# One core: q and k of eight early attention tiles come two tiles to a transfer and are turned by unit products

## The chip, the cores and the metric

The kernel runs on one core of a Trainium2 chip. The metric is the device time of one execution in microseconds (us), as a median of several runs. The engines are named as in the profile: PE (matrix products), DVE, ACT and POOL (elementwise work), SP (issues the transfers). "Granted clock" is the share of full speed that PE was given.

## The reference, cut to what matters

```python
# q, k, v: (8 batches, 8 heads, 576 tokens, 64)
scores = scale * q @ k.T                       # scale = 1/8
scores = where(0 <= row - col < 64, scores, -1e9)   # a token sees itself and 63 before it
attn = exp(scores - max); attn = attn / (sum + 1e-9)
x = (attn @ v) as (8, 576, 512)                # heads side by side
mixed = real(fft(fft(x, axis=1), axis=2))
u = x + mixed
un = (u - mean) / sqrt(var + 1e-6)             # per token
out = u + maximum(un @ w_ch1, 0) @ w_ch2       # 512 -> 2048 -> 512
```

## The kernel before

**Tiles.** The 8 x 576 tokens are cut into 36 tiles of 128 tokens, nine to a pair of batches. Tile 4 of a pair holds the last 64 tokens of one batch and the first 64 of the next. A tile goes through attention (`attn_tile`), its output is combined into four parts (`y`), turned, and folded into two transform stages for each batch (`fft`: tiles `pg`, `pz`), then normalized (`norm_tile`) and put through the two layers in chunks of two tiles (`ffn`, later `ffn7`: tiles `ph` and `po`, by far most of PE's work).

**Plain tiles.** Tiles 0 to 10 (`T < PRO`) are computed in whole 32-bit numbers, the others in pairs of 16-bit parts. For a plain tile `attn_tile` does this:

- `load` (line 538) brings k, q and v, each 128 tokens on 128 partitions, 8 heads of 64 numbers. In the source one token of one head is 256 contiguous bytes. The tiles `kn`, `qn` come from a ring of two; for odd tiles the second halves of `qbd` (`qbuf`) are used.
- `flip` (line 574) turns k and then q with four 128-column PE transposes each, into the PSUM tiles `pk` and `pq`; a copy (line 506 on ACT, line 510 on DVE) brings them into `kst` (three slots of one tile each) and `qbd` (two slots).
- `score` (line 662, tile `psc`) needs this tile's q, its k, and the k of the tile before it. Then masking on DVE (677), exponent on ACT (685), the turn of the result (696, `pp`, copied to `pt`), the product with v (739, `pa`, v in `va` and `ve`), and the division (747 to 758, into `xu`).

**Weights.** Both weight matrices come as 32 transfers of 512 KB (line 1277), each partition's piece being 4 KB contiguous, into `room` or `flex`, and DVE turns each two of them into `ws` by three instructions (1289, 1294, 1301). The slots of `ws` are free until then.

**Order.** Every step is recorded by `op` with the buffers that it reads and writes (`Buf`), which gives its dependences in the order of recording. The order of execution is then a table written into the source, `ORDER`; `SECOND` names the steps that run on their second engine. Each engine goes through its list strictly in order. All these loads are issued by SP. Where the planner's arithmetic sees PE idle for over 0.8 us before the first layer work, `WARM` has it fill the gap with products that nothing reads (line 1759, tile `warm`).

Of the kernel before, what the change touches and what calls it, by code (L numbers as in the profile page):

```python
# [27 lines left out]
P = 128  # L28
# [370 lines left out]
def attn_fft_ffn_kernel(ctx: ExitStack, tc: tile.TileContext, q, k, v, w1, w2, gidx, dft_d, dft_s, mask, out):  # L399
# [120 lines left out]
    def attn_tile(T, base):  # L520
# [36 lines left out]
        def keys(h, jj, rows):  # L557
# [6 lines left out]
            step = old - own  # L564
            return halves[rows, own : old + (1 if step > 0 else -1) : step]

        if whole:
            bpk, bpq = Buf("ps"), Buf("ps")

            def flip(dst, src):  # L570
# [1137 lines left out]
    for nth, (x, j) in enumerate(W_ORDER):  # L1708
        weight_pair(x, j, nth)
# [81 lines left out]
```

## Time and profile before

| what | value |
|---|---|
| median of 3 runs | 942.68 us (942.63 to 948.22) |
| the profiled execution, its own time | 945.16 us |
| its span, first to last instruction | 943.4 us |
| PE busy | 924.2 us (98%) |
| DVE, ACT, POOL busy | 705.3, 435.1, 441.5 us |
| warm products among PE's instructions | 45, the last at 40.9 us |

The span is what the rows divide up; 1.8 us of the execution's own time lie outside it, and this execution is 2.5 us above the median of the runs. The share of busy time is an average over stages: at the start, in the tail and in the middle PE waits for different things.

### The profile page before, as it was taken

The numbers are of one execution on the slowest core, as the hardware profiler recorded it, in microseconds if no ns is written. First come the engines' busy times: TensorE is split into PE (matmuls) and PEld (weight loads), VectorE is DVE, ScalarE is ACT, GpSimd is POOL, SyncE is SP. The second block draws the span as 40 slices with busy tenths as digits, with TensorE's granted clock in tenths as the row PEclk, the third lists the DMA queues.
The fourth block names the chain that finished last, engine by engine and source line by source line (L and its number), as shares of the span: only waits on it lengthen the run. The fifth ranks groups of instructions, "written<-read, shape, count | busy, mean of one in ns | idle before, by whom it ended". The sixth has DMA issues, their size and how long they took to land.

```text
span 943.4 us, 24809 instructions
## 1 busy us (share of the span) xinstructions
PE 924.2 (98%) x9717; PEld 703.2 (75%) x9717; DVE 705.3 (75%) x1982; ACT 435.1 (46%) x979; POOL 441.5 (47%) x823
## 2 busy tenths in 40 slices
PE   7799999999999999999999999999999999999998
PEld 6677777666766676666766676667779998888887
DVE  5898998887767866677658757888898965675664
ACT  6875777834555424445443543444334442422111
POOL 2653464744744555465746544655601454124012
PEclk9999999999999999999999999999999999999999
DMA  9997447999689969879979788785402032210100
GB/s 231 239 263 202 133 144 147 167 173 169 136 193 163 198 122 167 185 152 207 197 168 190 150 162 169 163 147 108 137 12 57 24 96 65 68 35 13 57 24 23
DMA packets 300230, 128.69 MB, mean 136 GB/s; under 512 B 277768, under 2 KB 278152, under 8 KB 300112
## 3 DMA queue, kind: packets, MB, share of 16 engines
q1 hardware_dynamic: 297248, 118.06, 59.6%
q0 software_dynamic: 2720, 8.92, 3.3%
q8 instruction: 76, 1.25, 0.6%
q14 instruction: 42, 0.34, 0.1%
q10 hardware_dynamic: 144, 0.13, 0.0%
HBM read 60.76 MB, written 19.94 MB: 86 GB/s over the span
## 4 chain that ended last, share of the span: by engine, by line
PE 83%; DMA 5%; DVE 4%; POOL 3%; SPq 2%; issue 2%; ACT 1%; POOLq 0%; DVEq 0%; ACTq 0%
PE ph L1419 22%; PE po L1400 22%; PE ph L1573 13%; PE po L1548 11%; PE pz L1061 3%; PE pg L1023 3%; PE pa L739 3%; PE psc L662 2%; DMA kn<-in_k 1%; POOL flex L516 1%; DMA ve<-va 1%; DMA qn<-in_q 1%; DMA pt<-flex 1%; SPq L1277 1%; PE py L850 1%
## 5 line engine op out<-in xcount | busy, mean ns | idle before, releaser
L1400 PE MATMUL po<-ws,hh 128*128 128x512 f16 (+1 forms) x1116 | 284.5, 391 | 0.5 <-issue 0.2
L1419 PE MATMUL ph<-room,ws 128*128 128x256 f16 x2112 | 256.1, 273 | 1.8 <-DVE hh L1431 1.8
L1419 PEld LDWEIGHTS <-ws 128*128 128x128 f16 x2112 | 205.3, 98 | 54.1 <-issue 2.8
L1400 PEld LDWEIGHTS <-hh 128*128 128x128 f16 x1056 | 101.1, 98 | 90.0 <-DVE hh L1431 0.7
L1573 PE MATMUL ph<-room,ws 128*128 128x256 f16 x1152 | 136.2, 273 | 0.0
L1573 PEld LDWEIGHTS <-ws 128*128 128x128 f16 x1152 | 112.6, 98 | 13.6
L1428 ACT ACTIVATE hh<-ph 128x512 f16<-128x512 f32 x88 | 52.3, 594 | 120.8 <-PE ph L1419 99.8
L685 ACT ACTIVATE pr<-pr,nm 128x128 f32<-128x128 f32 x288 | 91.2, 393 | 31.5 <-DVE nm L677 31.4
L1431 DVE SCALAR_TENSOR_TENSOR hh<-ph,hh 128x512 f16<-128x512 f32 x88 | 60.4, 686 | 36.6 <-ACT hh L1428 36.5
L1135 POOL DMA_INDIRECT mt<-md,gix x34 | 42.0, 1235 | 96.7 <-DVE mv L1163 81.5
L677 DVE CUSTOM_DVE_ANT_0 pr<-psc,mskb 128x128 f32<-128x128 f32 x288 | 65.0, 287 | 25.9 <-PE psc L662 19.7
L1584 ACT ACTIVATE hx<-ph 128x512 f32<-128x512 f32 x47 | 27.8, 595 | 113.3 <-PE ph L1573 103.7
L1589 DVE TENSOR_TENSOR hx<-hx 128x128 f32<-128x128 f32 x164 | 45.1, 318 | 37.8 <-ACT hx L1584 36.2
L1548 PEld LDWEIGHTS <-hh 128*128 128x128 f16 x658 | 64.4, 98 | 7.6
L1597 POOL TENSOR_TENSOR hl<-hx,hh 128x256 f16<-128x256 f32 (+1 forms) x40 | 28.0, 730 | 77.3 <-DVE hh L510 53.7
L516 POOL TENSOR_TENSOR up<-un,up 128x128 f16<-128x128 f32 x84 | 40.9, 516 | 46.3 <-ACT up L506 38.8
L516 POOL TENSOR_TENSOR flex<-pr,flex 128x128 f16<-128x128 f32 x92 | 42.5, 494 | 36.2 <-ACT flex L506 18.2
L1548 PE MATMUL po<-ws,hh 128*128 128x256 f16 x282 | 51.2, 273 | 0.0
L1597 DVE TENSOR_TENSOR hl<-hx,hh 128x896 f16<-128x896 f32 x37 | 40.4, 1097 | 7.8 <-ACT hh L506 6.5
L752 POOL TENSOR_TENSOR rc<-rc,mone 128x4 f32<-128x4 f32 x29 | 32.5, 1129 | 26.6 <-DVE rc L747 16.8
L739 PE MATMUL pa<-ve,pt 128*64 128x65 f16 (+1 forms) x776 | 37.0, 203 | 2.5 <-ACT ve L506 1.8
L1548 PE MATMUL po<-ws,hl 128*128 128x256 f16 x141 | 38.4, 273 | 0.0
(244 smaller groups left out, 1718.6 us busy)
## 6 DMA issues: line engine op xcount, KB each, us to landing
room<-in_moe_w_ch SPq DMA_DIRECT2D x20, 512.0 KB
flex<-in_moe_w_ch SPq DMA_DIRECT2D x12, 512.0 KB
ve<-va SPq DMA_DIRECT2D x47, 130.0 KB
flex<-in_v SPq DMA_DIRECT2D x22, 256.0 KB
xs<-xu SPq DMA_DIRECT2D x22, 256.0 KB
xv<-xs SPq DMA_DIRECT2D x22, 256.0 KB
out<-xv SPq DMA_DIRECT2D x21, 256.0 KB
md<-mp SPq DMA_DIRECT2D x24, 192.0 KB
```

Of the source, the lines that this page charges most:

```text
L516: eng.tensor_tensor(out=out[:, k : k + w], in0=in0[:, k : k + w], in1=in1[:, k : k + w], op=al)
L677: nc.vector.tensor_tensor_reduce(out=t["pr", g][:, hp], in0=t["ps", g][:, hp], in1=mskb[:, m : m + P], scale=-0.125, scalar=3.0e38, op0=AL ...
L685: nc.scalar.activation(pr, pr, AF.Exp, bias=t["nm", g][:, hp : hp + 1], scale=-1.0)
L739: nc.tensor.matmul(pa[sl, hp], pt[:, sl], v_, start=(x == 0), stop=(x == len(mm) - 1))
L1400: nc.tensor.matmul(t["po"][i], l_, r_, start=(f == 0 and x == 0), stop=(f == NKF - 1 and x == len(mm) - 1))
L1419: nc.tensor.matmul(ph, l_, r_, start=(x == 0), stop=(x == len(mm) - 1))
L1428: nc.scalar.activation(t["hh", j][:, 0], ph, AF.Relu)
L1431: nc.vector.scalar_tensor_tensor(out=hh[:, 1], in0=ph, scalar=0.0, in1=hh[:, 0], op0=ALU.max, op1=ALU.subtract)
L1548: nc.tensor.matmul(t["po", bk][:, x], t["h", j][a][:, slot], right(n, j, b_), start=(j == 0 and k == 0 and n in opens), stop=(j == seven - ...
L1573: nc.tensor.matmul(ph, l_, r_, start=(x == 0), stop=(x == len(mm) - 1))
L1589: eng.tensor_tensor(out=x[:, o], in0=x[:, p0], in1=x[:, p1], op=al)
L1597: eng.tensor_tensor(out=lo[:, a:b_], in0=x[:, a + 1 : b_ + 1], in1=hi[:, a:b_], op=ALU.subtract)
```

## The change

For tiles 0 to 3 and 5 to 8 (`twin`), two neighbouring tiles of one batch (0 and 1, 2 and 3, 5 and 6, 7 and 8) share one transfer of k and one of q (`two_tiles`). A partition receives two neighbouring tokens of each head, 512 contiguous bytes in the source, in 1024-number pieces of two `ws` slots (14 to 17 or 28 to 31, tile name `ws`). Since tokens 2p and 2p+1 then lie on one partition, the turn is done for even and for odd tokens apart (`turn_two`): per head one product with 64 stationary columns of data and the 128 x 128 unit matrix as moving operand, 8 products for one call, head by head into the lower and the upper 64 rows of the PSUM tile (`pt0...`, printed as `pt`). `spread_two` copies the result with a step of two columns into `kst` (both tiles' slots) or into both q slots. Each pair of tiles thus has 2 transfers in place of 4, 4 calls of `turn_two` in place of 4 of `flip`, and 4 copies as before. A pair's q needs both q slots free and a pair's k two of the three k slots.

The recording of weights, of the first layer chunk and of the normalization of tiles 0 to 8 moves behind tile 8, so that the weights' use of `ws` is ordered after the new use. `ORDER` and `SECOND` are new. Everything from about PE's row 2,470 of 17,388 on stands as before but for a few swaps.

```diff
-    qbuf = [cp.tile([P, 1024], F32, name=f"qbd{i}") for i in range(2)]
+    qboth = cp.tile([P, 2, 1024], F32, name="qbd")
+    qbuf = [qboth[:, i] for i in range(2)]
...
+        twin = T < NT and n != 4
+        if not twin:
+            bk, bq = Bkq if i else (Buf("kq"), Buf("kq"))
+            op("DMA", 1.45, base - 8, lambda: load("kn", "kq", k), writes=[bk], lat=2.0)
+            op("DMA", 1.45, base - 8, lambda: load("qn", "kq", q), writes=[bq], lat=2.0)
...
-        if whole:
+        if twin and n in (0, 2, 5, 7):
+            slot = (14, 30)[n in (2, 7)]
+            def two_tiles(x, src):
+                b_, s0 = b0 + P * n // S, P * n % S
+                rows = src[b_, :, s0 : s0 + 2 * P, :].rearrange("h (p i) d -> p h (i d)", i=2)
+                at = slot + (2 if slot == 14 else -2) * x
+                t["two", x] = ws[:, at : at + 2].rearrange("p i c -> p (i c)").rearrange("p (h i d) -> p h i d", h=H, i=2)
+                nc.sync.dma_start(t["two", x].rearrange("p h i d -> p h (i d)"), rows)
+            def turn_two(x, odd):
+                t["pt2", x, odd] = bank("ps", f"pt{x}{odd}_{T}")
+                for h in range(H):
+                    rows = slice(64 * (h % 2), 64 * (h % 2) + 64)
+                    nc.tensor.matmul(
+                        t["pt2", x, odd][rows, h // 2], t["two", x][:, h, odd], ident, start=True, stop=True
+                    )
+            def spread_two(eng, x, odd):
+                if x == 0:
+                    a, b_ = T % 3, (T + 1) % 3
+                    dst = kst.rearrange("p x (a s) -> p x a s", a=4)[:, a : b_ + 1 if b_ > a else None : b_ - a]
+                else:
+                    dst = qboth[:, :, 0:512].rearrange("p x (a s) -> p x a s", a=4)[:, :: 1 if i == 0 else -1]
+                copy(eng, dst[..., odd::2], t["pt2", x, odd].rearrange("p a (x s) -> p x a s", x=2))
+            for x, src in enumerate((k, q)):
+                bw = Bws[slot + (2 if slot == 14 else -2) * x :][0:2]
+                to = [BkT[T % 3], BkT[(T + 1) % 3]] if x == 0 else [Bq[0], Bq[1]]
+                op("DMA", 2.2, base - 8, lambda x=x, src=src: two_tiles(x, src), writes=bw, lat=2.0)
+                for odd in range(2):
+                    bpt2 = Buf("ps")
+                    op("PE", 1.0, base + 0.5 * x, lambda x=x, odd=odd: turn_two(x, odd), [*bw, Bid], [bpt2])
+                    op("ACT", 0.48, base + 0.1 + 0.5 * x, lambda e, x=x, odd=odd: spread_two(e, x, odd), [bpt2], to,
+                       alt=("DVE", 0.6), port=False)
+        elif twin:
+            pass
+        elif whole:
...
-        if T == 4:
+        if T == 8:
+            for nth, (x, j) in enumerate(W_ORDER):
+                weight_pair(x, j, nth)
+            for args in norms[:4]:
+                norm_tile(*args)
...
-1 115 0 9 7 116 3 15 118 119 120 145 121 124 144 129 16 149 125 130 173 126 131 147 150 117 127 148 17 132 21 18 176 153
...
```

Of the instructions, 64 one-record transposes (`pk`, `pq`; 16 calls of `flip`) become 128 unit products (16 calls of `turn_two`), and the 45 warm products become 28. In the changed file the lines are 538 and 578 (loads one by one, and by two), 584 (`turn_two`), 614 (`flip`), 702, 736, 779, 890 (scores, `pp`, `pa`, `py`), 1317 (weights) and 1806 (warm).

First SP, from its first transfer, before (`kn`, `qn` and `qbd` are the loads of k and q of tiles 0, 1 and 2; `room` is a weight transfer):

```order
L538 DMA kn_102<-in_k 128x8x64
L538 DMA qn_110<-in_q 128x8x64
L470 DMA mskb<-in_mask 128x384
L1277 DMA room<-in_moe_w_ch 128x1024
L538 DMA qbd_79<-in_q 128x8x64
L538 DMA qbd_78<-in_k 128x8x64
L1277 DMA room<-in_moe_w_ch 128x1024
L538 DMA kn_189<-in_k 128x8x64
L538 DMA va_82<-in_v 128x8x64
L1277 DMA room<-in_moe_w_ch 128x1024
L538 DMA qn_253<-in_q 128x8x64
```

The same stretch of SP now (the `ws` loads are of tiles 0 and 1, then of 2 and 3):

```order
L578 DMA ws<-in_k 128x8x128
L578 DMA ws<-in_q 128x8x128
L1317 DMA room<-in_moe_w_ch 128x1024
L470 DMA mskb<-in_mask 128x384
L578 DMA ws<-in_k 128x8x128
L1317 DMA room<-in_moe_w_ch 128x1024
L538 DMA va_81<-in_v 128x8x64
L538 DMA va_82<-in_v 128x8x64
L1317 DMA room<-in_moe_w_ch 128x1024
L578 DMA ws<-in_q 128x8x128
```

The q of tiles 2 and 3 stands behind both v loads and the third weight transfer, where the q of tile 2 alone stood behind one v load and the third weight transfer.

Then PE between the scores of tile 0 and those of tile 1, before:

```order
L574 MATMUL pq_175<-ident,qbd_79 128x128 x4
...
L696 MATMUL pp_1_197<-ident,pr_1_147 128x128 x4
L574 MATMUL pk_203<-ident,qbd_78 128x128 x4
L696 MATMUL pp_0_210<-ident,pr_0_145 128x128 x4
...
L574 MATMUL pk_226<-ident,kn_189 128x128 x4
L662 MATMUL psc_0_232<-kst,qbd_79 64x128 x2
```

The same stretch of PE now, up to the first product with v and the turns behind it (tile 1 needs no load and no turn of its own any more):

```order
L584 MATMUL pt_2_197<-ident,ws 64x128 x8
...
L736 MATMUL pp_1_225<-ident,pr_1_173 128x128 x4
...
L736 MATMUL pp_0_236<-ident,pr_0_171 128x128 x4
L702 MATMUL psc_0_245<-kst,qbd 64x128 x2
...
L779 MATMUL pa_0_271<-ve_83,pt_0_237 64x65
...
L584 MATMUL pt_2_302<-ident,ws 64x128 x8
L584 MATMUL pt_2_322<-ident,ws 64x128 x8
L584 MATMUL pt_2_340<-ident,ws 64x128 x8
```

The three flips between the two scores have gone; one turn of the next pair's k stands there, and its other three stand behind tile 0's product with v.

## Rows read from the trace of the kernel before

**Rows 1.** The page: span, PE's busy time, granted clock in 40 slices.

```profile
span 943.4 us, 24809 instructions
...
PE 924.2 (98%) x9717; PEld 703.2 (75%) x9717; DVE 705.3 (75%) x1982; ACT 435.1 (46%) x979; POOL 441.5 (47%) x823
...
PEclk9999999999999999999999999999999999999999
```

**Rows 2.** Stretches: each engine's busy us (instructions), granted clock, DMA share, GB/s.

```profile
core 0: us, PE busy (x) PEld busy (x) DVE busy (x) ACT busy (x) POOL busy (x), PEclk, DMA share, GB/s
0.00:8.20 8.20, 6.25 (x58) 4.83 (x58) 0.00 (x0) 2.46 (x3) 1.50 (x13) 1.00 0.80 184
8.20:50.00 41.80, 33.05 (x501) 25.40 (x498) 35.46 (x150) 34.21 (x87) 21.63 (x37) 1.00 1.05 254
50.00:200.00 150.00, 148.56 (x1302) 107.05 (x1302) 133.23 (x348) 106.81 (x230) 81.89 (x126) 1.00 0.71 170
90.00:110.00 20.00, 20.00 (x88) 14.44 (x86) 19.55 (x35) 12.95 (x26) 4.67 (x8) 1.00 0.39 132
```

**Rows 3.** The same stretches, the warm products of line 1759 alone.

```profile
0.00:8.20 8.20, 4.18 (x18) 2.39 (x18) 1.00 0.80 184
8.20:50.00 41.80, 4.63 (x27) 2.23 (x27) 1.00 1.05 254
```

**Rows 4.** PE's waits, 0 to 50 us: us in total, times, longest.

```profile
PE pa L739 <- ACT ve L506: 1.8, 3, 1.1
PE py L850 <- DVE y L516: 1.7, 2, 1.4
PE pk L574 <- DMA kn<-in_k: 1.5, 2, 1.3
PE psc L662 <- ACT qbd L506: 1.2, 2, 0.7
```

**Rows 5.** Timeline of PE: start us, us, instructions, [idle before, releaser].

```profile
4.45 1.06 PE L574 MATMUL pk<-ident,kn 128*128 128x128 f32 x4
...
7.19 1.10 PE L662 MATMUL psc<-kst,qbd 64*64 64x128 f32 x32 [0.46 <-ACT qbd L506]
...
9.49 0.63 PE L574 MATMUL pq<-ident,qbd 128*128 128x128 f32 x4 [0.77 <-DMA qbd<-in_q]
...
10.18 0.60 PE L696 MATMUL pp<-ident,pr 128*128 128x128 f32 x4
...
13.48 0.63 PE L574 MATMUL pk<-ident,kn 128*128 128x128 f32 x4 [1.28 <-DMA kn<-in_k]
...
17.72 0.63 PE L574 MATMUL pq<-ident,qn 128*128 128x128 f32 x4 [0.41 <-DMA qn<-in_q]
...
31.89 0.63 PE L574 MATMUL pk<-ident,kn 128*128 128x128 f32 x4 [0.18 <-DMA kn<-in_k]
```

**Rows 6.** Timeline of SP from 90 to 110 us: transfers issued.

```profile
91.23 0.80 SPq L1277 DMA_DIRECT2D room<-in_moe_w_ch  x2
96.26 0.81 SPq L1277 DMA_DIRECT2D flex<-in_moe_w_ch  x2
99.48 0.33 SPq L1277 DMA_DIRECT2D room<-in_moe_w_ch  x1
```

**Rows 7.** Chain that ended last, 46 to 92 us: start us, us, instructions.

```profile
48.81 1.03 PE psc L662 x32
...
51.82 1.08 PE pa L739 x32
...
59.73 0.44 PE pq L574 x4
...
88.93 1.73 PE ph L1419 x8
```

**Rows 8.** Groups by line and shape, 0 to 100 us: busy us, mean ns, idle.

```profile
L506 ACT COPY kst<-pk 128x512 f32<-128x512 f32 x11 | 6.4, 585 | 6.3 <-PE pk L574 6.2
...
L510 DVE COPY qbd<-pq 128x512 f32<-128x512 f32 x1 | 0.7, 692 | 0.1
```

More of the change, by code (lines that the diff above doesn't have):

```diff
@@ L538, in load @@
                 nc.sync.dma_start(t[nm][o : o + m], ap)
-        (bk, bq), bv = Bkq if i else (Buf("kq"), Buf("kq")), Bfl[3]
-        op("DMA", 1.45, base - 8, lambda: load("kn", "kq", k), writes=[bk], lat=2.0)
-        op("DMA", 1.45, base - 8, lambda: load("qn", "kq", q), writes=[bq], lat=2.0)
+        twin = T < NT and n != 4
+        bv = Bfl[3]
+        if not twin:
+            bk, bq = Bkq if i else (Buf("kq"), Buf("kq"))
+            op("DMA", 1.45, base - 8, lambda: load("kn", "kq", k), writes=[bk], lat=2.0)
+            op("DMA", 1.45, base - 8, lambda: load("qn", "kq", q), writes=[bq], lat=2.0)
         if whole:
@@ L1464, in attn_fft_ffn_kernel @@
         half[:, 4:6].rearrange("p i c -> p (i c)"),
-        *(b_[:].bitcast(F16) for b_ in qbuf),
+        *(b_.bitcast(F16) for b_ in qbuf),
         kst16[:, 0 : 2 * 1024],
@@ L1705, in ffn7 @@
             op("DMA", 0.75, -11, lambda g=g: nc.sync.dma_start(of[P * g : P * g + P], xts[g]), [b_], lat=2.0)
-    for nth, (x, j) in enumerate(W_ORDER):
-        weight_pair(x, j, nth)
-    made, behind = 0, {}
+    made, behind, norms = 0, {}, []
     for T in range(NTT):
@@ L1725, in attn_fft_ffn_kernel @@
                 else:
-                    norm_tile(*args)
-        if T == 4:
+                    norms.append(args)
+        if T == 8:
[3 more added lines that the diff above has]
+                norm_tile(*args)
+            del norms[:4]
             for c in range(PLAIN):
@@ L1734, in attn_fft_ffn_kernel @@
                     weight_split(x, j, W_SPLIT + W_STEP * 2 * (8 * x + j))
-        if n in (4, 8):
+        if n in (4, 8) and T > 4:
+            plan.slack = SLACK if T >= NT else 0.0
+            for args in norms:
+                norm_tile(*args)
+            norms.clear()
             plan.slack = FSLACK
```

276 rows, old and new, of tables (ORDER, SECOND) are left out of this document.

## The prediction

> **What bounds the kernel now.** I read the page first [rows 1]: a span of 943.4 us, 924.2 us of PE work, and the granted clock at full speed in every slice. Then the stretches [rows 2] say where PE is not the bound. In its first 50 us PE is idle for (8.20 - 6.25) + (41.80 - 33.05) = 10.7 us; from 50 to 200 us for 1.4 us. Against the span PE is idle for 943.4 - 924.2 = 19.2 us in all, so 8.5 us lie behind 50 us. In the first 50 us PE is also busy with warm products for 4.2 + 4.6 = 8.8 us [rows 3]. Empty time of the start, idle and warm together, is thus 6.1 us up to 8.2 us and 13.4 us from there to 50 us: 19.5 us. That is all that an earlier arrival of q and k can give back; behind 50 us PE has work queued whatever arrives.
>
> What PE waits for there is mixed [rows 4]: loads (k 1.5 us; one of q, 0.8 us, stands in [rows 5]), the copies of turned q on ACT (1.2 us), copies of v (1.8 us), and `y` on DVE (1.7 us). The transfer engines are full from 8 to 50 us (share 1.05), but DVE and ACT are busy for 35.5 and 34.2 of those 41.8 us as well [rows 2].
>
> **The queue.** From 90 to 110 us SP issues only five weight transfers [rows 6], and the engines' share is 0.39 [rows 2]: 0.39 x 20 / 5 = 1.56 us of all 16 engines for 512 KB in 4 KB pieces. Between the products that waited for tile 1's q, tile 2's k and tile 2's q, 4.0 and 4.2 us pass [rows 5], and each time, by SP's order shown with the change, the queue holds two loads of 256 KB and one weight transfer. One load of 1,024 pieces of 256 bytes so takes (4.1 - 1.56) / 2 = 1.27 us: 20 ns for a piece on one engine, against 195 ns for a piece of 4 KB. No row shows 512 bytes. On the straight line between the two prices a piece of 512 bytes takes 31.5 ns and a pair's transfer 2.02 us; at the 4 KB rate it would be 24.4 ns and 1.56 us. It replaces two loads, 2.54 us, so one of the eight new transfers frees 0.5 to 1.0 us of the queue, 4 to 8 us together. I take the straight line, since both ends of it are rows. The Trainium skill (DMA: Bandwidth & Descriptors, Specifications) says that pieces below 512 bytes miss the line rate because each is read and written back; by it the new transfers would cost the lower price and the queue would gain the 8 us. No run here shows it, and by the sum below the whole difference of 4 us in the queue is worth at most as much on PE.
>
> **Part 1, turns: PE work added.** A flip takes 0.44 us [rows 7]; 16 of them go: -7.0 us. A unit product is a plain 32-bit product, which the trace shows as two records: in the first layer 4 products of 256 columns are 8 records in 1.73 us [rows 7], 0.216 us for a record, 0.108 us for one of 128 columns. Alone, a call of 8 products would take 16 x 0.108 = 1.73 us. But the heads alternate between the two column halves, as the products with v do: those, with 64 stationary columns and 65 moving ones, take 1.08 us for 16 products in 32 records, 0.034 us a record where one alone would be 0.055. Perfect halves give 0.86 us for a call; scaling the product with v by columns (0.54 x 128 / 65) gives 1.06 us. The scores, with four places side by side, also need 1.03 / 32 = 0.032 us a record, so 0.033 us looks like a floor for small products, above which 0.054 us lies. I take 0.90 us. Added: 16 x 0.90 = 14.4 us. Together **+7.4 us** (16 x 0.42 = 6.7 to 16 x 0.62 = 9.9); without any overlap it would be +20.6 us. All of it lies on PE's own path; it is free only where it fills empty time.
>
> **Part 2, the first pair.** The first flip before stands at 4.45 us [rows 5], behind warm products. With 2.02 in place of 1.27 us, tiles 0 and 1's k is there at about 5.2 us and their q at 7.2 us. Two turns end at 9.0 us, the copy of q (0.69 us on DVE [rows 8]) at 9.7 us, and the scores run to about 10.8 us, where they ended at 8.2 us [rows 5]. Of these 10.8 us PE works 4 x 0.90 + 1.03 = 4.6 us, so 6.2 us stay empty against 6.1 us before. From scores to the first turned result 2.0 us pass (8.2 to 10.18 [rows 5]), of which one turn of the next k now fills 0.9 us. Tile 1 then needs neither load nor turn; its scores start after the two `pp` (0.9 and 0.4 us) at about 10.8 + 2.0 + 1.3 = 14.1 us, where the 13.48 us load let them start at 14.0 us [rows 5]. So the late start costs nothing from tile 1 on.
>
> **Part 3, the rest of the start.** Up to tile 2's q, which landed at 17.7 us [rows 5], SP's order before has 7 loads and 3 weight transfers, 7 x 1.27 + 3 x 1.56 = 13.6 us of queue; now it has 4 pair transfers, 2 loads and 3 weight transfers up to the q of tiles 2 and 3, 13.5 to 15.3 us: it lands at 17.6 to 19.4 us. Behind it come two weight transfers, tile 4's q, 0.5 MB of constants and tile 4's k, 2 x 1.56 + 2 x 1.27 + 1.5 = 7.2 us: 24.8 to 26.6 us against 31.9 us [rows 5]. Tiles 5 and 6, behind two v loads and two weight transfers, are there at 33.6 to 36.3 us. From tile 4 on the data is 5 us and more ahead, and PE meets its queued work from about 37 us instead of 50. What stays: a wait of up to 2 us for tiles 2 and 3, about 1 us in each of tiles 0, 2 and 3 between scores and turned results, where there is nothing else to do, and some of the waits for v and `y`, which the change doesn't touch. I put the empty time between 10.8 and 50 us at 5 us (2 to 9) in place of 13.4: **-8.4 us** (-11.4 to -4.4).
>
> **What costs nothing.** The copies stay 16; a stepped destination has no row, but ACT takes 585 ns for a contiguous one [rows 8] and 16 x 0.1 us would be spread over engines that do not end the stretch alone. The wait for both q slots holds back only the copies, with ACT and DVE's next steps behind them: the odd tile's scores are by then issued. The weights' move in the recording frees nothing and binds only four late transfers to the turns.
>
> **Sum.** +7.4 - 8.4 = -1.0 us on the span of 943.4: 942.4 us, and 944.2 us for that execution's own time, which lay 2.5 us above the median. On the median: 942.68 - 1.0 = **941.7 us**. The ends of the terms give 943.4 - 4.7 to 943.4 + 5.5, on the median 938.0 to 948.2.
>
> **Rivals.**
> 1. *The queue decides all of the start* (faster). If 512 bytes go at the 4 KB rate and the waits for v and `y` shrink with it, the 13.4 us fall to 1 us and a turn to 0.86 us: -12.4 + 6.7 = -5.7, and with another 1.5 us from the waits behind 50 us 935.5 us. For it: the share of 1.05 to 50 us. Against it: DVE and ACT are over 80% busy there, and DVE for 133 of the next 150 us [rows 2], so that work that arrives sooner finds them taken.
> 2. *The two column halves don't overlap* (slower). At `turn_two` PE then needs 1.73 us a call: +20.6 - 8.4 = +12.2, 954.9 us. It decides from a call of 0.44 + 8.4 / 16 = 0.97 us on; above that the change loses whatever the queue gains. Against it: the product with v has the same stationary shape and alternates in the same way, and overlaps.
> 3. *No relief.* The transfer is still cut into 256-byte pieces, or 512 bytes cost the double: the change then doesn't do what it says, the empty time stays at 19.5 us, and the turns are paid in full: 950.1 us. For it: nothing shows such a piece here. Against it: both sides of the transfer have 512 contiguous bytes.
> 4. *PE's strict order.* A turn stands ahead of tile 0's `pp`, three ahead of tile 1's; when a pair's load is late, everything behind waits though it could go. A queue that falls 2 us further behind costs up to 2 us at each of the two places: 945.7 us, inside the forecast's range.
>
> **How the numbers follow.** The forecast, with rival 4, has 0.69; rival 1 0.12; rival 3 0.10; rival 2 0.06; something else 0.03. Forecast and rival 1 hold 0.81 from 935.5 to 948.2 us; the bounds of the terms take in part of rival 3, so the range is 935 to 949 us. A measurement of this kernel can tell about 1%, 9.4 us, from no change. Even an empty time of zero behind the first 6 us would give -13.4 + 6.7 - 1.5 = -8.2 us, so faster by over 1% has 0.04; slower by over 1% is rival 2, the upper part of rival 3 and some of the rest, 0.10; within 1% 0.86.
>
> **What would show it.** In the changed profile: 8 transfers of 512 KB, DMA's packets below 512 bytes fewer by 16,384 and 8,192 of 512; records of the unit products starting about 0.055 us apart, a call 0.9 us; first scores ending near 11 us, tile 1's starting near 14 us; tile 4's k turned before 28 us; idle and warm together near 11 us in the first 50; and PE idle for less than 3 us from 50 to 200 us. I am wrong if a call takes over 1 us, if the pair's q of tiles 2 and 3 lands past 20 us, or if PE idles for more than 1 us at a time behind 50 us, for then DVE, not PE, sets that stretch.

## The result and the profile after

The changed kernel takes **948.12 us** (median of 20 runs, 944.74 to 953.76) where the kernel before takes 942.65 (20 runs): the ratio is 1.0053, 95% interval 1.0035 to 1.0071, some 5 us slower. I had forecast 941.7, 1 us faster. The size lies inside my range and inside the 1% that I gave 0.86; the sign is wrong.

The page of the changed kernel, span, engines and granted clock as in [rows 1]:

```profile
span 946.9 us, 25106 instructions
...
PE 931.3 (98%) x9892; PEld 709.1 (75%) x9892; DVE 710.2 (75%) x1984; ACT 432.6 (46%) x974; POOL 440.2 (46%) x814
...
PEclk9999999999999999999999999999999999999999
```

Its stretches, columns as in [rows 2], with 50 to 90 us apart (that row of the kernel before stands below them):

```profile
0.00:8.20 8.20, 6.78 (x64) 5.37 (x66) 0.00 (x0) 2.41 (x3) 1.64 (x14) 1.00 0.80 226
8.20:50.00 41.80, 35.76 (x609) 28.63 (x608) 34.55 (x147) 31.04 (x80) 22.58 (x36) 1.00 1.11 280
50.00:90.00 40.00, 38.00 (x398) 30.34 (x391) 33.41 (x97) 27.37 (x72) 29.57 (x45) 0.96 0.58 163
50.00:200.00 150.00, 147.48 (x1332) 106.55 (x1325) 131.70 (x327) 104.72 (x229) 88.33 (x133) 0.99 0.64 155
```

```profile
50.00:90.00 40.00, 39.64 (x406) 31.02 (x406) 36.11 (x125) 27.69 (x73) 22.06 (x34) 1.00 0.86 233
```

The warm products alone, now line 1806, split at the end of the first scores (compare [rows 3]):

```profile
0.00:10.80 10.80, 4.42 (x20) 1.00 0.87 255
10.80:50.00 39.20, 1.38 (x8) 1.00 1.11 275
```

The start did what it was to do. In the first 50 us PE is idle for 7.5 us and warm for 5.8 us, 13.3 us empty where it was 19.5 before; the transfer engines move 280 GB/s from 8 to 50 us where they moved 254. The new loss stands in the third row: from 50 to 90 us, where PE was idle for 0.4 us before, it is idle for 2.0 us, and the granted clock is 0.96 on average. PE's timeline has the two places where it waits longest, and the turns (compare [rows 5]):

```profile
5.38 4.03 PE L584 MATMUL pt<-ident,ws 128*64 128x128 f32 x64
10.29 1.10 PE L702 MATMUL psc<-kst,qbd 64*64 64x128 f32 x32 [0.56 <-DVE qbd L510]
...
14.55 1.30 PE L702 MATMUL psc<-kst,qbd 64*64 64x128 f32 x32
...
19.13 1.97 PE L584 MATMUL pt<-ident,ws 128*64 128x128 f32 x32 [0.58 <-DVE rc L787]
...
28.12 0.63 PE L614 MATMUL pk<-ident,kn 128*128 128x128 f32 x4 [1.89 <-DMA kn<-in_k]
...
77.51 0.94 PE L890 MATMUL py<-ident,y 128*128 128x128 f32 x4 [1.84 <-POOL y L516]
```

Four turns take 4.03 us and two take 1.97: 0.98 us a call, not 0.90. At 28.12 us PE has waited 1.89 us for tile 4's k; that flip stands in PE's order ahead of tile 3's scores, so everything behind waits too. At 77.51 it has waited 1.84 us for tile 6's sum on POOL. What follows the second wait shows in 1-us windows of PE (busy us, instructions, granted clock, DMA share, GB/s):

```profile
75.00:76.00 1.00, 0.67 (x7) 1.00 0.97 356
76.00:77.00 1.00, 0.00 (x0) 1.00 0.99 386
77.00:78.00 1.00, 0.49 (x3) 0.87 1.04 265
78.00:79.00 1.00, 1.00 (x15) 0.50 0.20 51
79.00:80.00 1.00, 1.00 (x28) 0.50 0.05 11
80.00:81.00 1.00, 1.00 (x12) 0.50 0.00 0
81.00:82.00 1.00, 1.00 (x15) 0.92 0.25 82
```

PE is busy but at 1.2 instead of 2.4 GHz for some 3.5 us: 0.13 + 3 x 0.5 + 0.08 = 1.7 us of work lost, as much as the wait itself. What PE waits for there is a sum on POOL. POOL's timeline before and then after (start us, us, instructions):

```profile
66.92 1.38 POOL L752 TENSOR_TENSOR rc<-rc,mone 128x4 f32<-128x4 f32 x1 [5.44 <-ACT rc L745]
...
71.89 1.89 POOL L516 TENSOR_TENSOR y<-xu 128x128 f32<-128x128 f32 x4
73.74 1.00 POOL L516 TENSOR_TENSOR y<-y 128x128 f32<-128x128 f32 x2
```

```profile
71.09 3.11 POOL L792 TENSOR_TENSOR rc<-rc,mone 128x4 f32<-128x4 f32 x2 [3.30 <-ACT rc L785]
74.80 1.71 POOL L516 TENSOR_TENSOR y<-xu 128x128 f32<-128x128 f32 x4 [0.60 <-PE mt L1142]
76.46 0.99 POOL L516 TENSOR_TENSOR y<-y 128x128 f32<-128x128 f32 x2
```

Each tile has two reciprocals, one for each half of its heads. Of tile 6's, one was on DVE; the new table of second engines leaves both on POOL. The second ends at 74.20 us, DVE's product with it at 74.65, the sum starts at 74.80 (a product of PE, which the row names, ends there too) and ends at 77.45 instead of 74.74. But tile 6's product with v had itself come 3 us later (from the chain that ended last: start us, us, what; before, then after):

```profile
64.89 1.17 PE pa L739 x32
```

```profile
67.97 1.08 PE pa L779 x32
```

From the end of that product to the end of the sum 8.7 us pass before (66.06 to 74.74) and 8.4 us now (69.05 to 77.45), so the moved reciprocal has not made this path longer. What has changed is how much work stands in PE's row between that product and the turn of the sum. Tile 8's scores (`psc`) and the turn (`py`) before, then tile 8's scores now:

```profile
73.48 1.10 PE L662 MATMUL psc<-kst,qbd 64*64 64x128 f32 x32
...
76.47 0.66 PE L850 MATMUL py<-ident,y 128*128 128x128 f32 x4
```

```profile
78.37 1.98 PE L702 MATMUL psc<-kst,qbd 64*64 64x128 f32 x32
```

Before, tile 8's scores and tile 7's products with v stood ahead of the turn; now they stand behind it. PE came to the turn 10.4 us after tile 6's product with v, with the sum ready; now it comes there after 6.6 us, at 75.67, and stands until 77.51. So the new order of PE made this hole; a path shorter by 1.8 us, with fewer steps on POOL, would have fitted into what is left. No run moved the turn back alone.

The reason for the other wait is SP's order (start us, us in SP's queue):

```profile
12.02 0.43 SPq L578 DMA_DIRECT2D ws<-in_q  x1
12.50 0.81 SPq L1317 DMA_DIRECT2D room<-in_moe_w_ch  x1
13.35 1.51 SPq L538 DMA_DIRECT2D qn<-in_q  x2
14.91 1.78 SPq L473 DMA_DIRECT2D ds__77<-in_dft_s  x1
16.74 0.43 SPq L1317 DMA_DIRECT2D flex<-in_moe_w_ch  x1
17.21 1.29 SPq L538 DMA_DIRECT2D kn<-in_k  x2
```

Tile 4's k goes out at 17 us, 8 us sooner than before, but behind a constant of 481 KB and a weight transfer, and lands at 28.0.

**The sum in the two traces**: turns 16 x (0.98 - 0.44) = +8.6, empty time of the first 50 us -6.2, idle time from 50 to 90 us +1.6, half clock +1.7: +5.7 us. I check it on a product that both kernels come to in the same order, the first scores at 247.47 us before; in the changed kernel:

```profile
253.08 0.25 PE L702 MATMUL psc<-kst,qbd 64*64 64x128 f16 x4
```

That is +5.6 us. (The spans differ by only 3.5 us because the profiled execution of before, 2.5 us above its median, lost time further on that this one did not: from 100 to 450 us PE was idle for 3.4 us in it, for 1.1 us here.) Below, "the mark" is this product's start, against 247.47.

### The profile page after: what moved, and what is told of

Same layout as the page of the kernel before. It is cut to its first block, busy times and chain, and to the rows that moved or that the text cites. A ratio compares the mean times of both kernels' runs of the same rounds, so it can differ in the third digit from the quotient of the medians.

```text
span 946.9 us, 25106 instructions
## 1 busy us (share of the span) xinstructions
PE 931.3 (98%) x9892; PEld 709.1 (75%) x9892; DVE 710.2 (75%) x1984; ACT 432.6 (46%) x974; POOL 440.2 (46%) x814
## 2 busy tenths in 40 slices
DMA packets 291911, 128.71 MB, mean 136 GB/s; under 512 B 261256, under 2 KB 269832, under 8 KB 291792
## 4 chain that ended last, share of the span: by engine, by line
PE 85%; DMA 4%; DVE 4%; POOL 3%; SPq 2%; ACT 1%; issue 1%; ACTq 0%; POOLq 0%; DVEq 0%
PE ph L1459 24%; PE po L1440 23%; PE ph L1613 13%; PE po L1588 11%; PE pz L1101 3%; PE pg L1063 3%; PE pa L779 3%; PE psc L702 3%; POOL y L516 1%; DMA kn<-in_k 1%; SPq L538 1%; DMA pt<-flex 1%; DVE y L516 1%; SPq L1317 1%; PE py L890 1%
## 5 line engine op out<-in xcount | busy, mean ns | idle before, releaser
L516 POOL TENSOR_TENSOR up<-un,up 128x128 f16<-128x128 f32 x80 | 37.9, 503 | 44.2 <-ACT up L506 36.7
L792 POOL TENSOR_TENSOR rc<-rc,mone 128x4 f32<-128x4 f32 x36 | 41.8, 1169 | 32.5 <-DVE rc L787 19.3
L516 POOL TENSOR_TENSOR flex<-pr,flex 128x128 f16<-128x128 f32 x80 | 36.5, 486 | 26.1 <-ACT flex L506 18.4
L1216 POOL TENSOR_SCALAR rs<-mv 128x1 f32<-128x1 f32 x36 | 11.8, 328 | 71.4 <-ACT un L1210 69.5
L516 POOL TENSOR_TENSOR flex<-qbd,flex 128x128 f16<-128x128 f32 x68 | 33.7, 527 | 18.1 <-ACT flex L506 18.0
```

The lines of the kernel that those rows point to most:

```text
L516: eng.tensor_tensor(out=out[:, k : k + w], in0=in0[:, k : k + w], in1=in1[:, k : k + w], op=al)
L792: eng.tensor_tensor(out=rc, in0=rc, in1=mone, op=ALU.pow)
```

## The experiments

Theory A: the turns are paid on PE's path. Theory C: tile 6's wait for POOL and the half clock behind it. Theory D: the new table as a whole. Theory F: tile 4's late k. All ratios are against the kernel before on the same chip; they need not equal the quotient of two medians.

**Turns alone**, in the kernel before:

```diff
 def flip(dst, src):
+    if T < NT and n != 4:   # 8 products of 64 stationary columns, as in turn_two
+        for h in range(H): nc.tensor.matmul(t[dst][rows, h // 2], t[src][:, h], ident, ...)
+        return
```

> The kernel before, with one thing taken from the change: in tiles 0 to 3 and 5 to 8 each flip of four 128-column transposes is now the eight 64-column unit products of the turns. Transfers, order and the engines of all steps stay. Theory A (the turns are paid on PE's path, 0.98 us for a call in the trace of the changed kernel against 0.44 us): 16 calls add 8.6 us of PE work; before tile 5 some of it fills time in which PE was empty anyway, so +4 to +8 us, 947 to 951 us. Theory B (the turns hide and the loss is all in the new order's steps on POOL): within 1.5 us of the kernel before.

Measured: 947.48 us, ratio 1.0038 (1.0020 to 1.0056), that is +3.6 us (1.9 to 5.3); the mark at 250.41, +2.9. In the old order less than half of the 8.6 us comes through, a little under theory A's +4 and well over theory B.

**The wide pieces undone**, in the changed kernel:

```diff
-nc.sync.dma_start(t["two", x].rearrange("p h i d -> p h (i d)"), rows)
+for i_ in range(2):
+    nc.sync.dma_start(t["two", x][:, :, i_], rows[..., i_])   # 256-byte pieces
```

> The changed kernel, but each pair's transfer is issued as two, one for the even and one for the odd tokens of the partitions, so that the pieces are 256 bytes again; order, turns and copies stay. If the wider pieces relieve the queue and PE lives on that in the first 50 us (my prediction's Part 3), the relief of 0.5 to 1.0 us for each of eight transfers goes: tile 4's k lands 4 us later and the time rises by 2 to 6 us, to 950 to 954 us. Rival (data that comes earlier brings no tile earlier, since POOL's and DVE's steps end the waits from 30 us on): within 1.5 us of the changed kernel's 948.

Measured: 953.76 us, 1.0103 (1.0073 to 1.0132), apart from the changed kernel's interval: 5.6 us more by the medians. The transfers of the first 50 us, the changed kernel first, then this one:

```profile
DMA packets 18802, 13.55 MB, mean 271 GB/s; under 512 B 8724, under 2 KB 17031, under 8 KB 18794
```

```profile
DMA packets 23741, 11.72 MB, mean 234 GB/s; under 512 B 22096, under 2 KB 22224, under 8 KB 23735
```

The wider pieces do relieve the queue, and this order lives on it: no loss comes from there. (The run also issues twice as many of these transfers, so it tests size and number together. In this trace PE waits 3.7 us for tile 4's k, and the granted clock is 0.50 from 30 to 36 us, so part of the 5.6 us is clock.)

**Tile 7's steps on DVE**, the three added to the table of second engines:

> The changed kernel with three steps of tile 7 on DVE in place of POOL: its two reciprocals and its sum of four halves (the table of second engines gets 270, 274 and 276). In the changed kernel's trace PE waits for that sum for 1.84 us at 75.7 us, and from 77 to 82 us its granted clock is at half speed. Theory C (this wait and the half clock behind it cost 1.8 + 1.6 us): the wait and the fall go, and the time falls by 2 to 3.5 us to 945 to 946 us. Rival (the slack is taken up further on): within 1 us of 948.

Measured: 949.62 us, 1.0057 (1.0030 to 1.0085). I had named the wrong tile: the product at 77.5 us is tile 6's. The wait (1.9 us) and the half clock behind it are still in the trace, so the run says nothing of theory C.

**Tiles 5 to 7 on DVE**, nine steps:

> The changed kernel with the reciprocals and the sums of tiles 5, 6 and 7 on DVE in place of POOL, nine steps. In the changed kernel's trace the chain from 31 to 43 us goes through two such sums on POOL of 3 us each and two reciprocals of 1 us. Theory C (POOL's slow small steps, which the new table of second engines uses more often, set the tiles' pace from 30 to 80 us): the time falls by 4 us or more, to 944 us or less. Rival (DVE is as busy, so the work only changes its queue): as the run with tile 7's steps alone, or slower.

Measured: 945.38 us, 1.0027 (1.0008 to 1.0045); the mark at 248.78, +1.3; PE busy for 39.40 of the 40 us from 50 to 90 at a clock of 1.00. The direction is theory C's, the size 1.4 us short of it, and the interval still overlaps the changed kernel's.

**Tile 6 alone on DVE:**

> The changed kernel with the two reciprocals and the sum of tile 6 alone on DVE. The run that was meant to take away PE's wait at 75.7 us moved tile 7's steps, and its trace still shows the wait (1.9 us) and the half clock behind it: the sum that PE waits for there is tile 6's. Theory C, restated (this one wait and the half clock behind it cost the changed kernel about 3 us, and tile 6's three steps are the part that counts of the run with tiles 5, 6 and 7 on DVE, 945.4 us): 945 to 946 us, with the granted clock at 1.00 from 50 to 90 us. Rival (that run's gain comes from tiles 5 and 7 or from all nine steps together): 947.5 us or more.

Measured: 946.72 us, 1.0048 (1.0028 to 1.0067): by the time alone not to be told from the changed kernel. The trace agrees with the theory where it speaks: no wait for `y` above 0.2 us from 50 to 90 us, clock 1.00, and from tile 7's scores to tile 9's 22.2 us pass instead of 24.8. The path from tile 6's product with v to its sum is down to about 7.0 us (69.9 to 76.84); the planner, which now sees a gap ahead of the turn, fills what is left of it with two warm products at 76.34 us. So do the later runs with these steps on DVE. But this execution waited 1.7 us for tile 4's k and then ran at half clock from 28 to 31 us. That second hole led to theory F.

**Cheap turns**, in the changed kernel:

```diff
+if h < 2: nc.tensor.matmul(t["pt2", x, odd][rows, h // 2], t["two", x][:, h, odd], ident, ...)
+else:     nc.tensor.matmul(t["pt2", x, odd][rows, h // 2], ident16[:, 0:64], ident16[:, 0:128], ...)
```

> The changed kernel with a turn's price on PE taken down to about that of a flip: of the eight unit products of a call two stay as they are, and six multiply constants in 16 bits, so that six of eight heads of q and k in these tiles are not the reference's; transfers, order and copies stay. Theory A (the 16 turns are paid on PE's path: 0.98 against 0.44 us for a call, of which 4 of 8.6 us came through in the kernel before with unit products alone): 943 to 945 us. If all 8.6 us are paid here: 940 us. Rival (PE only waits where the turns now stand): 947 us or more.

Measured: 950.07 us, 1.0082 (1.0060 to 1.0104): not faster. In its windows of PE, where turns that end sooner leave PE idle, the clock falls:

```profile
18.00:20.00 2.00, 1.62 (x21) 0.66 1.23 206
20.00:22.00 2.00, 2.00 (x12) 0.50 1.09 221
26.00:28.00 2.00, 0.00 (x0) 1.00 1.08 262
28.00:30.00 2.00, 1.43 (x8) 0.72 1.05 264
```

Tile 4's k lands at 28.5 us here, no sooner than with full turns. Theory A fails for this order, though the half clock hides by how much.

**The old order** with the new transfers and turns:

> The changed kernel in the order of the kernel before: every step that both kernels have stands where it stood and runs on the engine that it had, a pair's two transfers stand where the first tile's loads stood, its turns and copies where the first tile's flips and copies stood. Theory D (the new table of order and second engines brings what is lost beyond the turns, the wait of 1.8 us and the half clock of 1.6 us at 76 us among it): no half clock, and 944 to 946.5 us. Rival E (the new table is what makes the pairs bearable: in the old one the first tile's scores wait for 512 KB where they waited for 256 KB, and weights sit in the queue ahead of the pairs): 949 us or more.

Measured: 947.23 us, 1.0050 (1.0030 to 1.0070), between both: theory D falls as I put it. (The trace is of the slowest of the six runs, 952.6 us.) No half clock shows, but from 8.2 to 50 us the engines' share is 0.82 instead of 1.11 and PE spends 9.1 us on warm products in the first 50: the old order leaves the queue's gain unused.

**All of tiles 0 to 8 on DVE**, 17 steps:

> The changed kernel with all reciprocals and sums of tiles 0 to 8 on DVE that stood on POOL, 17 steps. If POOL's slow steps still hold tiles 0 to 4 back (the chain of waits of the run with tiles 5 to 7 on DVE still goes through two sums on POOL from 29 to 38 us): 1 us or more below that run's 945.4. Rival (in the first 50 us DVE is busy for 36 of 42 us, so it becomes what the tiles wait for): above 945.4.

Measured: 945.61 us, 1.0039 (1.0024 to 1.0053): no gain over nine steps. DVE is busy for 37.9 of the 41.8 us from 8.2 to 50 us: the rival.

**Tile 4's k early**, one number moved in the order table:

```diff
-... 76 78 128 44 57 ... 59 132 127 45 89 ...
+... 76 78 128 127 44 57 ... 59 132 45 89 ...     # 128: q of tile 4, 127: its k
```

> The changed kernel with one transfer moved in SP's order: tile 4's k stands right behind tile 4's q, ahead of a constant of 481 KB and a weight transfer of 512 KB, behind which the new order has put it. Theory F (the queue's gain was spent on the constant and the weights; tile 4's k lands at 28.1 us and PE waits 1.7 to 2.8 us for it in the traces of the changed kernel and of the runs with tile 6's steps on DVE and with cheap turns): it lands about 3 us earlier, PE's wait for it goes, tile 4's scores start near 27 us, and the time falls by 1 to 2 us, to 946 to 947 us. Rival (the steps on POOL and DVE hold tiles 4 and 5 anyway): tile 5's scores start at 43 us or later as before, and the time stays at 948.

Measured: 946.76 us, 1.0031 (1.0015 to 1.0047); the mark at 251.00, 2.1 us earlier than in the changed kernel. By the time alone the two can't be told apart: the intervals overlap. PE's timeline has no wait for k any more (the scores are tile 3's, where the expectation names tile 4's):

```profile
26.10 0.66 PE L622 MATMUL pk<-ident,kn 128*128 128x128 f32 x4
...
27.67 1.10 PE L710 MATMUL psc<-kst,qbd 64*64 64x128 f32 x32
```

Of the 2.1 us the moved load brings 1.2: tile 7's scores start at 64.60 us instead of 65.82. The rest comes where this execution, too, waits 1.82 us for tile 6's sum but keeps its full clock behind it, which the edit doesn't explain.

**Warm products in the second hole:**

```diff
+if o.idx == 244:      # tile 6's turn of y
+    for _ in range(8): nc.tensor.matmul(warm, wide[:, 0:P], wide, start=True, stop=True)
```

> The changed kernel with eight warm products ahead of the product that waits for tile 6's sum at 75.7 us, so that PE works through the 1.8 us in which it waited. The wait stays as long as it was. If the half clock from 77 to 82 us follows from the pause: the granted clock is 1.00 from 70 to 90 us, tile 9's scores start 1.6 us earlier, and the time falls by 1 to 1.6 us, to 946.5 to 947. Rival (the clock falls for another cause): 0.5 in that stretch again, and 948.

Measured: 945.38 us, 1.0007 (0.9988 to 1.0027), apart from the changed kernel's interval; the medians on this chip are 2.0 us apart (943.38 before). Its timeline shows the eight products and what is left of the wait; its clock is 1.00 throughout:

```profile
74.89 1.04 PE L1809 MATMUL warm<-ident 128*128 128x256 f16 x8
...
76.87 0.66 PE L890 MATMUL py<-ident,y 128*128 128x128 f32 x4 [0.94 <-POOL y L516]
```

```profile
76.00:77.00 1.00, 0.13 (x1) 1.00 1.12 326
77.00:78.00 1.00, 1.00 (x24) 1.00 0.50 118
```

Work that computes nothing, in a hole that stays, gives back time: this agrees with a half clock that follows the pause. The gain by the medians (2.7 us) is over the 1.6 us of the theory; of the 3.0 us by which the mark comes earlier 0.6 stood already at tile 5's scores, ahead of the edit, and 1.3 come at the hole (tile 9's scores start at 88.72 us instead of 90.66), so that the runs' own spread is in it.

**Both holes filled**, tile 4's k early and tile 6's three steps on DVE:

> Both holes filled: tile 4's k moved as in the run with that alone, and tile 6's two reciprocals and its sum on DVE. If the two holes and the half clocks behind them are what the changed kernel loses beyond its turns (theories C and F): 943.5 to 945.5 us, and the granted clock is 1.00 in every stretch. Rival (one of the two holes is only moved on to the next late step): not below the better of the two single runs, about 946.

Measured: 943.78 us, **1.0004 (0.9991 to 1.0018)**, apart from the changed kernel's interval and not to be told from the kernel before. The mark is at 248.56, +1.1. Its stretches:

```profile
8.20:50.00 41.80, 37.24 (x648) 30.02 (x646) 35.44 (x149) 32.16 (x81) 23.81 (x39) 1.00 1.06 282
50.00:90.00 40.00, 39.49 (x437) 31.46 (x434) 37.06 (x103) 27.43 (x72) 26.82 (x37) 1.00 0.62 178
```

**Tiles 5 and 7 on DVE as well:**

> As the run with both holes filled (tile 4's k early, tile 6's steps on DVE, 943.8 us), with tile 5's and 7's reciprocals and sums on DVE too. If POOL's small steps set more than the one wait of tile 6: 942.5 us or less, below the kernel before. If the one wait was all: 943 to 945 us, the same as with tile 6's steps alone.

Measured: 944.23 us, 1.0004 (0.9988 to 1.0020): no further gain shows; of the nine steps tile 6's three are enough.

**Both holes filled and cheap turns** (the edit of the first run with cheap turns):

> As the run with both holes filled, with turns at about a flip's price: six of a call's eight products multiply constants in 16 bits, so that six of eight heads of q and k in tiles 0 to 3 and 5 to 8 are not the reference's. If all 16 turns lie on PE's path, as my Part 1 has it, 8 us go: 936 us. If about half of it fills time in which PE waits anyway, as the kernel before with unit products alone suggests (4 of 8.6 us): 939 to 941 us. If copies, sums and transfers set the pace of the tiles up to tile 8 whatever PE does: 943 us or more, with the saved time as idle time of PE in the first 90 us.

Measured: 944.95 us, 1.0006 (0.9985 to 1.0028): the third case. Calls at half the price bring nothing that can be measured, where the intervals leave room for 2 to 3 us and not for 8; in the trace the mark moves by 1.7 us, to 246.89. Its stretch from 8.2 to 50 us:

```profile
8.20:50.00 41.80, 32.62 (x568) 26.36 (x569) 35.07 (x153) 32.13 (x81) 24.56 (x40) 0.96 1.09 290
```

From 8.2 to 50 us PE is busy for 4.6 us less than with full turns, and tile 6's scores start only 0.8 us sooner. Here, too, the clock falls, from 19 to 22 us, behind waits of 0.8 and 1.1 us; by the average clock of 0.96 that takes back some 1.7 us.

**Pairs for tiles 0 to 3 alone**, `twin = T < NT and n < 4`, the places of the separate loads and flips of tiles 5 to 8 put into the table by me:

> Pairs for tiles 0 to 3 alone: tiles 5 to 8 get their k and q as before, one transfer for each and flips of 0.44 us, in the changed kernel's order otherwise, with tile 4's k early and the reciprocals and sums of tiles 5 to 7 on DVE. Eight turns less are 8 x 0.54 = 4.3 us of PE work less, most of it in a stretch where PE has no empty time. Theory A for the later pairs (their turns are paid in full and their transfers buy nothing): 940 to 942 us, below both kernels. Rival (the queue needs the later pairs too, and tiles 5 and 6 wait for data): 944 us or more.

Measured: 946.82 us, 1.0024 (1.0004 to 1.0043), a miss. The trace has a wait of 2.0 us for `y` on DVE and a stretch of half clock in the first 50 us, so my table made a hole of its own; whether the later pairs are worth their turns stays open. No version tried beats the kernel before.

## Why the prediction was wrong

The balance that I struck, turns against queue, was about right in its sum, in part by luck, since neither side was all that I took it for (Part 1 below): with the two holes filled the change costs +0.4 us by the ratio (-0.8 to +1.7) where I had -1.0. The 5 us are two waits that the new table of order and second engines makes, with the half clock behind one or both.

- **"Behind 50 us PE has work queued whatever arrives" failed.** I read the changed table as the means to move loads and turns, and priced nothing else that it moved; "What costs nothing" did not name it. It put the turn of tile 6's sum ahead of tile 8's scores and tile 7's products with v, so that PE comes to it 6.6 us after tile 6's product with v instead of 10.4, while the sum on POOL takes 8.4. PE stood for 1.84 us in its row and then lost 1.7 us at half clock in this trace (the runs with tile 6 on DVE, with warm products, and with both holes filled take the wait or the half clock away). The prediction's sign of being wrong, PE idle for over 1 us at a time behind 50 us, came true, but not because DVE sets that stretch.
- **Part 3, tile 4's k at 24.8 to 26.6 us, failed.** It lands at 28.0. From the landing of q of tiles 2 and 3, in by 19.1 us as forecast (17.6 to 19.4), I gave the five loads up to it 7.2 us; they took 8.9 or more. Nor did I ask what in PE's order stands behind that flip: tile 3's scores do. It is rival 4's mechanism at a place that I had not looked at. Moving that load alone brought tile 7's scores forward by 1.2 us.
- **The queue** gave what was forecast: packets below 512 bytes fell from 277,768 to 261,256 (16,512; forecast 16,384), and between 512 bytes and 2 KB they rose from 384 to 8,576 (8,192, as forecast). Rival 3, no relief, is out by the run with narrow pieces.
- **Part 1**: a call is 0.98 us, not 0.90, so +8.6 and not +7.4; inside my bounds. But "all of it lies on PE's own path" is wrong: with the holes filled, calls of half the price brought 1.7 us of 8.6. Up to tile 6 the turns stand where PE would wait for copies, sums and loads, and they keep it busy, and in both runs with cheap turns the clock fell to half from about 19 to 22 us. So the break-even of 0.97 us in rival 2 was no break-even: both sides of that sum, turn time and empty time, are largely the same microseconds.
- **Part 2** held: first scores end at 11.4 us (forecast 10.8), tile 1's start at 14.55 (14.1). ACT's stepped copy takes 0.63 us where the contiguous one took 0.585 [rows 8]: 16 x 0.05 us, nothing.
- **Empty time** from 10.8 to 50 us is 5.5 idle + 1.4 warm = 6.9 us, not 5, inside 2 to 9; of the 6.2 us regained in the first 50 none is left when the turns are paid, and tile 6's scores start at 49.75 us against 48.74.

What stays open: how much of the loss each hole has. The single runs overlap in their intervals (1.0031 for tile 4's k, 1.0048 for tile 6's steps, 1.0007 for warm products). With both holes filled nothing of the loss is left, but the run with warm products alone can't be told from the kernel before either, so it is not shown that both were needed. Why the clock falls behind some of these waits and not behind others is open too.

## What to carry to other kernels

When a change brings a new table of order or of engines, go through every step that it moves, not only those it was written for. For each product that waits for other engines, compare the work that stands ahead of it in the bound engine's row with the time that the other engines take: here 6.6 us of work against a path of 8.4. A relief of the queue is worth what is put at its head: look what stands between the relieved transfers and the next load that the bound engine meets in its row. And before work is charged to a bound engine's path, ask whether it fills a wait there: if so, making it cheaper gives idle time back and no microseconds.

## What the runs showed of the hardware

The same pause of PE does not always cost the same. Behind tile 6's wait of 1.8 to 1.9 us the granted clock fell to 0.50 for about 3 us in the traces of the changed kernel and of the run with tile 7's steps, yet in the run with tile 4's k early it stayed at 1.00:

```profile
74.00:75.00 1.00, 0.44 (x5) 1.00 0.98 377
75.00:76.00 1.00, 0.00 (x0) 1.00 1.01 370
76.00:77.00 1.00, 0.74 (x8) 1.00 0.91 209
77.00:78.00 1.00, 1.00 (x33) 1.00 0.03 7
```

Likewise behind tile 4's k: none after 1.89 us in the changed kernel, half clock after 1.7 us in the run with tile 6 on DVE. Such a hole costs its own length in one execution and about twice that in another. And a reciprocal of four numbers a partition takes 1.0 to 2.1 us on POOL (1.38 in the row at 66.92 us above, 3.11 for the two at 71.09), while DVE's take 0.18 us (at 26.12 and 26.86 us in the changed kernel's trace).
